# Four conditional parts instead of two arms for seven of the eight experts, and every block sends its own output

## The chip, the cores and the metric

One core of a Trainium2 chip runs the kernel. The time is what the device needs for one execution, in microseconds, as the median of several runs. Beside the timed runs there is one profiled execution, from which all rows below are taken. PE is the matrix engine (TensorE), PEld its weight loads, DVE is VectorE, ACT is ScalarE, POOL is GpSimd and SP is SyncE, which here only starts transfers.

## The reference

The work is a chunked attention, a dense two-layer network and a mixture of eight experts, one after the other. The change touches the mixture alone:

```python
    logits = x @ w_gate
    expert_idx = np.argmax(logits, axis=1)
    ...
    gate_w = probs[np.arange(N), expert_idx]
    ...
        if counts[e] < capacity:
            disp[e, counts[e]] = x[i]
            ...
    h = np.maximum(np.einsum('ecd,edf->ecf', disp, w1), 0.0)
    y = np.einsum('ecf,efd->ecd', h, w2)
    ...
            out[i] = gate_w[i] * y[expert_idx[i], pos[i]]
```

N is 1536 tokens, D 512, F 1024, and the capacity of an expert 384 tokens. So an expert has up to three blocks of 128 tokens. How many tokens it really gets is known only when the kernel runs.

## The kernel before, in words

Every f32 operand is held as a high and a low part, and a product is made of three matmuls (high by high, high by low, low by high). The experts run in the order of `EORDER`; the number e below counts in that order, from 0. The first expert (e = 0) has code of its own (`after_first`, L990), which the change does not restructure. For e = 1 to 7 the loop at L1245 writes two arms under `tc.If(cnt[EORDER[e]] > P)` (L1260):

- The arm `more` (L1006) is for over 128 tokens. `layer1` (L847) runs for eight pieces of F over both blocks together: 96 matmuls of 256 columns, each piece evacuated by ACT (L861, the high part of `hT`) and then by DVE (L862, the low part). `next_trans` (L974) then transposes both blocks of the next expert on PE (L825, 8 transposes), which ACT (L829) and DVE (L830) copy out as the high and low part of `xs`. `layer2(0)` follows: 24 matmuls of 512 columns (L925). Then comes `rest(2)` (L958) with a second `tc.If` (L963): over 256 tokens, the arm transposes block 2, runs `layer2(1)` and then the whole of block 2 (`block`, L866); else the arm runs `layer2(1)` alone.
- The arm `one` (L985) is for up to 128 tokens: `block(0)` with its 24 matmuls of 512 columns in layer 1 (L880), eight transposes of `hs` (L889), 24 matmuls of layer 2 (L925), and `next_trans` in its midst.

The last block of either arm does not send its result. It leaves it in one PSUM tile, copies its gate and its rows' numbers to two small tiles on POOL (L938, L939), and `after_arms` (L955) behind both arms sends it: ACT scales it (L945) and POOL starts an indirect transfer (L946). An earlier block of an arm sends its own.

In the same arms the weights of the coming steps are split into their high part (ACT, L289) and low part (DVE, L294), eight pieces for each expert: four of this expert's w2 and four of the next expert's w1. In `more` the eight stand in one stretch of code with layer 1, in `one` they stand between the steps of the block.

Which expert takes which arm can be read from the trace by the tiles: e = 1 takes `more` with block 2 (365.32 to 402.24 us), e = 2 takes `one` (405.14), e = 3 `more` (419.82), e = 4 `one` (444.63), and e = 5, 6 and 7 take `more` (461.56, 485.12, 508.75).

Order and waits: a planner (Tile) orders the instructions of one arm freely by their priorities, but moves nothing into or out of an arm. Each engine runs its own instruction stream, with its own branch at each condition, and counts its finished work in one counter of its own; who needs a result waits until the counter of its producer has reached a number. The numbers go on through the program as it is written. An arm that is not taken leaves a hole in them, and the engine itself fills it: where it passes such an arm without other work in it, it first waits until its own earlier work is done and then adds the missing count in one step. For the two arms of one If and Else the numbers run side by side, and the first instruction of the shorter arm adds the difference.

On PE a matmul is two instructions, a weight load and a multiplication. In the text of the program the arm `more` up to L963 has 256 such instructions, the arm of L963 168, its else 48, and `one` 128.

Of the kernel before, what the change touches and what calls it, by code (L numbers as in the profile page):

```python
# [9 lines left out]
F32 = mybir.dt.float32  # L10
# [3 lines left out]
I32 = mybir.dt.int32  # L14
# [7 lines left out]
P = 128  # L22
# [21 lines left out]
EORDER = (1, 2, 0, 3, 4, 5, 6, 7)  # L44
# [43 lines left out]
def kernel(  # L88
# [14 lines left out]
    nc = tc.nc  # L103
# [246 lines left out]
    def w_state():  # L350
        return w_at[0], list(flight), list(free_slots), list(free_raw), dict(where), set(ready)
# [46 lines left out]
    def psum(kind, name):  # L398
        pool, tag, shape = ps_pools[kind]
        return pool.tile(shape, F32, tag=tag, name=name)  # L400
# [399 lines left out]
    def expert_parts(e, ep, tp, cnt):  # L800
# [32 lines left out]
        def gate(b):  # L833
            sm = tp.tile([P, 1], F32, tag="gs", name="gs")
            nc.scalar.activation(out=tp.tile([P, E], F32, tag="ex", name="ex"), in_=xr[b][:, DM:DM + E], func=AF.Exp, accum_out=sm)  # L835
            g = tp.tile([P, 1], F32, tag="gt", name="gt", bufs=8)
            nc.vector.tensor_scalar(out=sm, in0=sm, scalar1=EPS, scalar2=None, op0=ALU.add)
            nc.vector.reciprocal(out=g, in_=sm)
            gt[b] = g

        def hT_of(b):
            key = 0 if b < 2 else b
# [23 lines left out]
        def block(b, last, pump=lambda i: None, between=None):  # L866

            with in_order():
# [42 lines left out]
                pump(5)  # L911
                layer2_part(b, p2, range(4, F2))
                pump(6)
            evacuate(b, p2, last)

        def y_of(last):
            return ylast[0] if last else psum("y", "psy")

        def layer2_part(b, ps, fcs):
            h = hT[0 if b < 2 else b]  # L920
# [7 lines left out]
        def layer2(b, last):  # L928
            ps = y_of(last)
            layer2_part(b, ps, range(F2))  # L930
            evacuate(b, ps, last)

        ylast = []

        def evacuate(b, ps, last):
            if last:

                nc.gpsimd.tensor_copy(ylast[1], gt[b])  # L938
                nc.gpsimd.tensor_copy(ylast[2], taker[:, b, ex:ex + 1])  # L939
            else:  # L940
                send(ps, gt[b], taker[:, b, ex:ex + 1])

        def send(ps, g, place):
            y = ep.tile([P, DM], F32, tag="y", name="y", bufs=2)
# [4 lines left out]

        def before_arms():  # L950
            hT_of(0)
            ylast.extend([psum("yl", "psy"), tp.tile([P, 1], F32, tag="gl", name="gl"),
                          tp.tile([P, 1], I32, tag="tl", name="tl")])

        def after_arms():  # L955
            send(*ylast)

        def rest(b):  # L958

            if b == NCB:  # L960
                layer2(b - 1, True)
                return
            with tc.If(cnt[ex] > b * P) as more:  # L963
                trans(b)
                layer2(b - 1, False)
                gate(b)
                later(b)
            with more.Else():
                layer2(b - 1, True)

        def later(b):
            block(b, True)

        def next_trans():  # L974
            if e + 1 < E:
                parts[e + 1].trans(0)
                parts[e + 1].trans(1)
# [28 lines left out]
        def more():  # L1006

            for b in range(2, NCB):
                load(b)
            for fc in range(F2):  # L1010
                mm, act = layer1(fc)
                if fc == GFC:
                    after_act = act
                if fc == TFC:
                    after_mm = mm
                if fc in PUMPS:
                    w_next(e)
            with tc.issue_after(after_act):
                for b in range(2):
                    gate(b)  # L1020
            with tc.issue_after(after_mm):
                next_trans()
            layer2(0, False)
            with tc.high_priority(offset=-LOWER2):
                while w_next(e):
                    pass
            rest(2)
        return SimpleNamespace(load=load, trans=trans, xs_of=xs_of, one=one, more=more, after_first=after_first,
                               before_arms=before_arms, after_arms=after_arms)


    with ExitStack() as st:
# [187 lines left out]
    with ExitStack() as st:  # L1220
# [24 lines left out]
        for e in range(E):  # L1245
            if e + 1 < E:
                for b in range(2):
                    parts[e + 1].load(b)
                parts[e + 1].xs_of(0)
            if e == 0:  # L1250
                with tc.high_priority(offset=LOADS):
                    w_loads(8 * (F // 512))
                first_block.send()
                parts[0].after_first()
            else:
                parts[e].before_arms()
                with tc.high_priority(offset=LOADS):
                    w_loads(8 * (F // 512))
                before = w_state()
                with tc.If(cnt[EORDER[e]] > P) as full:  # L1260
                    parts[e].more()
                after = w_state()
                w_back(before)
                with full.Else():
                    parts[e].one()
                assert w_state() == after
                parts[e].after_arms()
            for j in range(F // 512):
                w_free(("w1", e, j))
            for j in range(F // 512):  # L1270
                w_free(("w2", e, j))
# [70 lines left out]
```

## Time and profile before

| | |
|---|---|
| median of 3 runs | 540.67 us (539.94 to 542.19) |
| profiled execution, its own time | 540.01 us |
| its span, first to last instruction | 538.2 us |
| time around the span | 1.8 us |
| PE busy | 516.9 us (96%) |
| DVE, ACT, POOL busy | 311.0, 272.6, 85.1 us |
| mean granted clock of PE | 0.991 |

Of the profile, the busy shares and the forty slices say which engine sets the pace; the table of stretches says the same for each expert; the timeline of PE shows where it stands still (the idle time before a line, and who ended it, in square brackets); a line's own view shows the branch and counter instructions of each engine's sequencer (PEldq, ACTq and so on), with the shortest, median and longest duration in ns.

### The profile page before, as it was taken

How to read it: one execution, taken by the hardware profiler on the slowest of the kernel's cores; microseconds unless marked ns; L12 is line 12 of the kernel's file. 1: busy time of each engine (PE TensorE's matmuls, PEld its weight loads, DVE VectorE, ACT ScalarE, POOL GpSimd, SP SyncE). 2: the span in 40 equal slices, each digit the busy share in tenths (PEclk: the TensorE clock that was granted, in tenths of full speed). 3: DMA queues.
4: the chain of work that ended last, by engine and by line, in shares of the span. 5: the costliest groups of instructions: out<-in, count | busy, mean ns of one | idle time of the engine just before them, and what ended most of it. 6: DMA issues, size and time to landing. Idle time of an engine off the chain costs nothing. (4 is left out here: it accounts for less than half of the span.)

```text
span 538.2 us, 10665 instructions
## 1 busy us (share of the span) xinstructions
PE 516.9 (96%) x4211; PEld 445.0 (83%) x4211; DVE 311.0 (58%) x627; ACT 272.6 (51%) x551; POOL 85.1 (16%) x92
## 2 busy tenths in 40 slices
PE   8898999999999999999999999999988997999995
PEld 4686888899988999889988887779777976989893
DVE  4899799995229722228375446457314944947250
ACT  2786879773237422235254334457235925938231
POOL 3211012222001100004100000232022222201111
PEclk9999999999999999999999999999998998999999
DMA  8985654342003530000168213597524884885000
GB/s 287 328 315 193 238 174 141 120 158 79 1 0 119 184 130 1 1 0 2 37 210 264 80 41 98 161 319 260 181 62 160 269 324 146 279 328 196 23 26 31
DMA packets 38955, 80.29 MB, mean 149 GB/s; under 512 B 4009, under 2 KB 10153, under 8 KB 38890
## 3 DMA queue, kind: packets, MB, share of 16 engines
q1 hardware_dynamic: 36010, 70.66, 38.3%
q0 software_dynamic: 2880, 8.74, 5.1%
q8 instruction: 43, 0.70, 0.5%
q14 instruction: 22, 0.18, 0.1%
HBM read 69.90 MB, written 10.27 MB: 149 GB/s over the span
## 5 line engine op out<-in xcount | busy, mean ns | idle before, releaser
L584 PE MATMUL acc<-w,g 128*128 128x512 f32 x576 | 153.3, 400 | 1.1 <-DVE w L294 0.7
L541 PEld LDWEIGHTS psh<-xT,w 128*128 128x128 f32 x1152 | 146.7, 188 | 7.4
L541 PE MATMUL psh<-xT,w 128*128 128x256 f32 x1152 | 151.1, 280 | 0.0
L584 PEld LDWEIGHTS acc<-w,g 128*128 128x128 f32 x576 | 100.6, 188 | 21.5 <-issue 2.1
L556 ACT ACTIVATE sg<-psh 128x256 f32<-128x256 f32 x96 | 36.8, 384 | 128.2 <-PE psh L541 127.8
L294 DVE TENSOR_TENSOR w<-raw,w 128x1024 fp32r<-128x1024 f32 x64 | 77.2, 1220 | 41.5 <-ACT w L289 38.0
L564 DVE TENSOR_TENSOR g<-sg,g 128x256 fp32r<-128x256 f32 x87 | 40.3, 463 | 77.8 <-ACT g L560 74.7
L925 PE MATMUL psy<-w,hT 128*128 128x512 f32 x336 | 82.7, 400 | 0.3 <-ACT y L945 0.3
L925 PEld LDWEIGHTS psy<-w,hT 128*128 128x128 f32 x336 | 62.0, 188 | 15.3 <-ACT y L945 0.6
L289 ACT ACTIVATE w<-raw 128x1024 fp32r<-128x1024 f32 x64 | 66.3, 1060 | 2.8 <-PE acc L584 2.2
L858 PEld LDWEIGHTS psh<-xs,w 128*128 128x128 f32 x480 | 58.0, 188 | 1.1 <-issue 0.7
L858 PE MATMUL psh<-xs,w 128*128 128x256 f32 x480 | 58.3, 282 | 0.3 <-PEq L1000 0.3
L560 ACT ACTIVATE g<-psh 128x256 fp32r<-128x256 f32 x96 | 36.2, 380 | 0.0
L595 DVE SCALAR_TENSOR_TENSOR x<-acc,x 128x512 f32<-128x512 f32 x36 | 24.3, 687 | 18.2 <-PE acc L584 18.0
L880 PE MATMUL psh<-w,xs 128*128 128x512 f32 x96 | 27.4, 438 | 7.0 <-ACT w L289 2.9
L880 PEld LDWEIGHTS psh<-w,xs 128*128 128x128 f32 x96 | 19.6, 210 | 12.7 <-issue 7.2
L808 POOL DMA_INDIRECT xr<-rows,taker x20 | 24.2, 1211 | 23.6 <-DVE w L294 16.9
L294 DVE TENSOR_TENSOR w<-w,w 128x512 fp32r<-128x512 f32 x27 | 21.6, 802 | 9.5 <-ACT w L289 9.3
L270 DVE SCALAR_TENSOR_TENSOR w<-raw,w 128x512 int32<-128x512 int32 x32 | 23.4, 734 | 0.1
L259 ACT ACTIVATE w<-raw 128x512 f32<-128x512 f32 x32 | 21.1, 670 | 1.4 <-DMA raw<-in_w_out_dram 1.2
L289 ACT ACTIVATE w<-w 128x512 fp32r<-128x512 f32 x32 | 20.0, 628 | 3.5 <-POOL w L284 2.0
L284 POOL TENSOR_TENSOR w<-w,rest 128x512 int32<-128x512 int32 x8 | 12.1, 1507 | 60.8 <-DVE w L270 55.0
(134 smaller groups left out, 487.2 us busy)
## 6 DMA issues: line engine op xcount, KB each, us to landing
raw<-in_w_dram SPq DMA_DIRECT2D x64, 512.0 KB, 5.0
raw<-in_w_in_dram SPq DMA_DIRECT2D x16, 512.0 KB, 3.8
raw<-in_w_out_dram SPq DMA_DIRECT2D x16, 512.0 KB, 3.3
vt<-in_v_dram SPq DMA_DIRECT2D x12, 512.0 KB, 3.6
kt<-in_k_dram SPq DMA_DIRECT2D x12, 368.0 KB, 6.7
qt<-in_q_dram SPq DMA_DIRECT2D x12, 256.0 KB, 4.1
out_dram<-blank SPq DMA_DIRECT2D x12, 256.0 KB, 4.2
rows<-x SPq DMA_DIRECT2D x5, 520.0 KB, 4.1
```

Source lines behind the costliest of these rows:

```text
L289: nc.scalar.activation(out=w_dst(self.name, self.i, 0), in_=w, func=AF.Copy)
L294: eng.tensor_tensor(out=lo, in0=w, in1=hi.bitcast(F32), op=ALU.subtract)
L541: nc.tensor.matmul(ps, lhsT=w[:, wz, c, i * P:(i + 1) * P], rhs=xT[tb][:, xz, c, :], start=n == 0, stop=n == 3 * KC - 1)
L556: nc.scalar.activation(out=sg_t[u], in_=h_t[u], func=AF.Silu, scale=1.702)
L560: g_last[:1] = [nc.scalar.activation(out=g[:, 0], in_=h_t.pop(u), func=AF.Silu, scale=1.702).ins]
L564: lo = eng.tensor_tensor(out=g[:, 1], in0=sg_t.pop(u), in1=g[:, 0].bitcast(F32), op=ALU.subtract)
L584: nc.tensor.matmul(acc_t[tb][s], lhsT=g[:, gz, s * P:(s + 1) * P], rhs=w[:, wz, wi, :], start=i == 0 and n == 0, stop=u == last_of(k, tb) ...
L595: nc.vector.scalar_tensor_tensor(out=dst, in0=acc_t[tb][s], scalar=1 / 1.702, in1=dst, op0=ALU.mult, op1=ALU.add)
L808: return nc.gpsimd.indirect_dma_start(out=t, out_offset=None, in_=rows[:, :], in_offset=bass.IndirectOffsetOnAxis(ap=taker[:, b, ex:ex + 1 ...
L858: mm = nc.tensor.matmul(ps, lhsT=w[:, wz, c, f0:f0 + P], rhs=t[:, xz, c, :], start=m == 0, stop=m == 3 * KC - 1)
L880: nc.tensor.matmul(p1[j], lhsT=x[:, xz, c, o:o + P], rhs=w[:, wz, c, :], start=(xz, wz, c) == (0, 0, 0), stop=(xz, wz, c) == (1, 0, KC - 1))
L925: nc.tensor.matmul(ps, lhsT=h[:, hz, fc, o:o + P], rhs=w[:, wz, fc % 4, :], start=fc == 0 and n == 0, stop=fc == F2 - 1 and n == 2)
```

## The change

The two arms of e = 1 to 7 become four conditional parts in a row, none of them with an Else:

1. over 128 tokens: `more`, now only layer 1, the gates and `next_trans`;
2. up to 128 tokens: `one`, as it was;
3. over 128 tokens: `more2`, that is `layer2(0)`, the rest of the weights and `layer2(1)`;
4. over 256 tokens: `rest`, that is the transposes, the gate and the whole of block 2.

Each block sends its own output in its own part, so `ylast`, `after_arms` and the two copies on POOL go. The tiles for the gates are made ahead of the parts (`gt_of`). Six of the eight weight pieces of an expert with over 128 tokens now stand in `more2`, two in `more`.

```diff
-            g = tp.tile([P, 1], F32, tag="gt", name="gt", bufs=8)
+            if b not in gt:
+                gt_of(b)
...
         def y_of(last):
-            return ylast[0] if last else psum("y", "psy")
+            return psum("yl" if last else "y", "psy")
...
-        def evacuate(b, ps, last):
-            if last:
-
-                nc.gpsimd.tensor_copy(ylast[1], gt[b])
-                nc.gpsimd.tensor_copy(ylast[2], taker[:, b, ex:ex + 1])
-            else:
-                send(ps, gt[b], taker[:, b, ex:ex + 1])
+        def evacuate(b, ps):
+            send(ps, gt[b], taker[:, b, ex:ex + 1])
...
-        def after_arms():
-            send(*ylast)
-
-        def rest(b):
-
-            if b == NCB:
-                layer2(b - 1, True)
-                return
-            with tc.If(cnt[ex] > b * P) as more:
-                trans(b)
-                layer2(b - 1, False)
-                gate(b)
-                later(b)
-            with more.Else():
-                layer2(b - 1, True)
-
-        def later(b):
-            block(b, True)
+            for b in range(NCB):
+                gt_of(b)
...
+        def more2():
+
             layer2(0, False)
             with tc.high_priority(offset=-LOWER2):
                 while w_next(e):
                     pass
-            rest(2)
+            layer2(1, True)
+
+        def rest():
+
+            for b in range(2, NCB):
+                with tc.If(cnt[ex] > b * P):
+                    trans(b)
+                    gate(b)
+                    block(b, b % 2 == 1)
...
-                with tc.If(cnt[EORDER[e]] > P) as full:
+                with tc.If(cnt[EORDER[e]] > P):
                     parts[e].more()
+                middle = w_state()
+                w_back(before)
+                with tc.If(cnt[EORDER[e]] < P + 1):
+                    parts[e].one()
                 after = w_state()
-                w_back(before)
-                with full.Else():
-                    parts[e].one()
+                w_back(middle)
+                with tc.If(cnt[EORDER[e]] > P):
+                    parts[e].more2()
                 assert w_state() == after
-                parts[e].after_arms()
+                parts[e].rest()
```

`w_state` and `w_back` only keep the book of the weight tiles while the program is written: `one` and `more2` write and read the same tiles.

## Rows read from the trace of the kernel before

**Rows 1.** The page: busy time of the engines; PE's granted clock in 40 slices.

```profile
PE 516.9 (96%) x4211; PEld 445.0 (83%) x4211; DVE 311.0 (58%) x627; ACT 272.6 (51%) x551; POOL 85.1 (16%) x92
...
PEclk9999999999999999999999999999998998999999
```

**Rows 2.** Stretches, PE alone: length, busy (matmuls), granted clock, DMA share, GB/s.

```profile
405.14:409.40 4.26, 4.26 (x12) 0.60 0.60 189
...
419.82:443.62 23.80, 23.80 (x153) 1.00 0.90 307
443.62:447.38 3.76, 0.47 (x1) 0.95 0.38 109
447.38:450.40 3.02, 3.02 (x8) 0.50 0.78 227
...
485.12:508.75 23.63, 23.63 (x153) 1.00 0.37 124
```

**Rows 3.** Timeline of PE: start, length, instructions, idle time before and its releaser.

```profile
365.32 11.69 PE L858 MATMUL psh<-xs,w 128*128 128x256 f32 x96 [0.32 <-PEq L1000]
...
390.00 4.36 PE L880 MATMUL psh<-w,xs 128*128 128x512 f32 x18
...
405.14 5.99 PE L880 MATMUL psh<-w,xs 128*128 128x512 f32 x18 [2.91 <-ACT w L289]
...
444.63 0.47 PE L880 MATMUL psh<-w,xs 128*128 128x512 f32 x1 [1.01 <-ACT y L945]
447.38 5.47 PE L880 MATMUL psh<-w,xs 128*128 128x512 f32 x17 [2.28 <-issue]
```

**Rows 4.** Lines L1260 and L963: branches of PE's sequencer, ns min/median/max, first and last start.

```profile
L1260 PEldq COMPARE_BRANCH  x1: 5036/5036/5036, 399.9 to 399.9; - x1
...
L1260 PEldq COMPARE_BRANCH  x1: 2974/2974/2974, 441.5 to 441.5; - x1
...
L963 PEldq COMPARE_BRANCH  x10: 65/294/2167, 379.4 to 527.2; - x10
```

**Rows 5.** Waits of POOL: who waited for whom, total us, times, longest.

```profile
POOL out_dram L946 <- ACTq L963: 56.0, 4, 15.0
```

**Rows 6.** Timeline of all engines around the transposes for the next expert, e = 0.

```profile
361.15 1.03 PE L825 MATMUL pst<-ident,xr 128*128 128x128 f32 x8
361.79 1.09 ACT L829 ACTIVATE xs<-pst 128x512 fp32r<-128x512 f32 x2 [1.24 <-PE pst L825]
...
361.94 3.06 PE L925 MATMUL psy<-w,hT 128*128 128x512 f32 x12
362.42 1.29 DVE L830 TENSOR_TENSOR xs<-pst,xs 128x512 fp32r<-128x512 f32 x2 [0.95 <-ACT xs L829]
```

**Rows 7.** Timeline where layer 1 of the last expert (e = 7) ends.

```profile
520.18 11.40 PE L925 MATMUL psy<-w,hT 128*128 128x512 f32 x48
520.38 0.39 ACT L861 ACTIVATE hT<-psh 128x256 fp32r<-128x256 f32 x1 [1.03 <-PE psh L858]
520.80 0.42 DVE L862 SCALAR_TENSOR_TENSOR hT<-psh,hT 128x256 fp32r<-128x256 f32 x1 [0.99 <-ACT hT L861]
```

**Rows 8.** Timeline where the two `one` experts end (e = 2, then e = 4).

```profile
418.88 5.76 DVE L294 TENSOR_TENSOR w<-raw,w 128x1024 fp32r<-128x1024 f32 x5
...
420.61 0.69 ACT L945 ACTIVATE y<-psy,gl 128x512 f32<-128x512 f32 x1
...
460.60 5.77 DVE L294 TENSOR_TENSOR w<-raw,w 128x1024 fp32r<-128x1024 f32 x5
461.56 8.67 PE L858 MATMUL psh<-xs,w 128*128 128x256 f32 x71
```

**Rows 9.** Timeline at the start of block 2 of e = 1.

```profile
383.34 0.60 PE L825 MATMUL pst<-ident,xr 128*128 128x128 f32 x4
383.54 0.69 ACT L945 ACTIVATE y<-psy,gt 128x512 f32<-128x512 f32 x1 [4.97 <-PE psy L925]
...
384.31 0.59 ACT L829 ACTIVATE xs<-pst 128x512 fp32r<-128x512 f32 x1
```

More of the change, by code (lines that the diff above doesn't have):

```diff
@@ L835, in gate, with gt_of @@
             nc.scalar.activation(out=tp.tile([P, E], F32, tag="ex", name="ex"), in_=xr[b][:, DM:DM + E], func=AF.Exp, accum_out=sm)
-            g = tp.tile([P, 1], F32, tag="gt", name="gt", bufs=8)
+            if b not in gt:
+                gt_of(b)
             nc.vector.tensor_scalar(out=sm, in0=sm, scalar1=EPS, scalar2=None, op0=ALU.add)
-            nc.vector.reciprocal(out=g, in_=sm)
-            gt[b] = g
+            nc.vector.reciprocal(out=gt[b], in_=sm)
+        def gt_of(b):
+            gt[b] = tp.tile([P, 1], F32, tag="gt", name="gt", bufs=9)
         def hT_of(b):
@@ L913, in block @@
                 pump(6)
-            evacuate(b, p2, last)
+            evacuate(b, p2)
         def y_of(last):
-            return ylast[0] if last else psum("y", "psy")
+            return psum("yl" if last else "y", "psy")
         def layer2_part(b, ps, fcs):
@@ L930, in layer2 @@
             layer2_part(b, ps, range(F2))
-            evacuate(b, ps, last)
-        ylast = []
-        def evacuate(b, ps, last):
-            if last:
-                nc.gpsimd.tensor_copy(ylast[1], gt[b])
-                nc.gpsimd.tensor_copy(ylast[2], taker[:, b, ex:ex + 1])
-            else:
-                send(ps, gt[b], taker[:, b, ex:ex + 1])
+            evacuate(b, ps)
+        def evacuate(b, ps):
+            send(ps, gt[b], taker[:, b, ex:ex + 1])
         def send(ps, g, place):
@@ L951, in before_arms @@
             hT_of(0)
-            ylast.extend([psum("yl", "psy"), tp.tile([P, 1], F32, tag="gl", name="gl"),
-                          tp.tile([P, 1], I32, tag="tl", name="tl")])
-        def after_arms():
-            send(*ylast)
-        def rest(b):
-            if b == NCB:
-                layer2(b - 1, True)
-                return
-            with tc.If(cnt[ex] > b * P) as more:
-                trans(b)
-                layer2(b - 1, False)
-                gate(b)
-                later(b)
-            with more.Else():
-                layer2(b - 1, True)
-        def later(b):
-            block(b, True)
+            for b in range(NCB):
+                gt_of(b)
         def next_trans():
@@ L1026, in more @@
                     pass
-            rest(2)
-        return SimpleNamespace(load=load, trans=trans, xs_of=xs_of, one=one, more=more, after_first=after_first,
-                               before_arms=before_arms, after_arms=after_arms)
+            layer2(1, True)
[5 more added lines that the diff above has]
+                    block(b, b % 2 == 1)
+        return SimpleNamespace(load=load, trans=trans, xs_of=xs_of, one=one, more=more, more2=more2, rest=rest,
+                               after_first=after_first, before_arms=before_arms)
     with ExitStack() as st:
```

## The prediction

> **What bounds the kernel now.** I read the page first, then the stretches, the timeline of PE, the branches, and last who waits for whom. The page says that PE is busy for 96% of the span, the next engine for 58%, and that the granted clock is full but for two dips [rows 1]. So only what stops or slows PE counts. The stretches show where the experts lose: one with over 128 tokens loses nothing (23.80 us busy of 23.80, 23.63 of 23.63), while the entry into the second `one` expert is 3.76 us with a single matmul in it, followed by 3.02 us at half clock; after the entry into the first `one`, 4.26 us have a mean clock of 0.60 [rows 2]. The timeline gives the idle times: 2.91 us ahead of the first `one` (e = 2); 1.01 and 2.28 us around the one matmul ahead of the second (e = 4) [rows 3]. The clock costs more on top: 18 of these matmuls take 4.36 us at full clock (0.242 each) and 5.99 us after the first stop, so 1.6 us; 17 take 5.47 us after the second, where 4.1 would do, so 1.4 us [rows 3]. The two entries together: 6.2 us idle and 3.0 us of slow clock, 9.2 us.
>
> What stops PE there is no missing result, though the profile names ACT: the weights and `xs` of these experts were made during the expert before. PE's own branch at L1260 took 5.04 us at e = 2 and 2.97 us at e = 4, while its ten branches at L963 take 0.07 to 2.17 us, half of them under 0.3 [rows 4]. Both long ones jump over the whole arm `more`, 472 PE instructions as counted in the program; the ordinary ones jump over 130 to 170. [...]
>
> **The change part by part.** I add to the profiled execution, 540.0 us; the median of the runs shown is 0.7 us higher.
>
> *Shorter jumps.* The way into `one` now leads over `more` without its second half, 208 instructions, and then past empty parts. That is nearer to the ordinary jumps than to the 472, so I take their cost (a median of 0.29 us [rows 4], spent while earlier matmuls still run) and remove all 9.2 us. Bounds: nothing removed, and all of it. What is late next is a wait: `one` is preceded by `more` passed over, and PE's first matmul takes a PSUM tile last read in `more`, so it needs ACT's count for that part. ACT passes it only after it has scaled the last output, about 0.15 + 0.69 us after PE's end (the wait of 1.01 us that is there already [rows 3] has this length). I put 1.0 us at each of the two entries, 2.0.
>
> *The wait between the two halves.* This is the main term. `layer2(0)` reads `hT`. Before, only `more` wrote it ahead of `layer2(0)`. Now `one` is written between them in the program and writes the same `hT` and the same weight tiles, so the wait of `layer2(0)` is for numbers of ACT and DVE that belong to `one`. Where `one` isn't taken, ACT and DVE add these numbers when they have passed it, after all of their work in `more`. That such a count is waited for shows before: POOL waited 56.0 us in four waits for ACT's sequencer at L963, a condition and no work [rows 5]. The last work in `more` is copying the transposes of `next_trans`. Before, 24 matmuls of layer 2 ran on while this was done; behind the matmuls that now wait stand all of layer 2 and the next expert. Counted from the first transpose at 361.15, ACT is done at 362.88 (+1.73) and DVE at 363.71 (+2.56), while PE went on with other matmuls at 361.94 (+0.79) [rows 6]. With 0.1 us for the signal PE can run one matmul (0.24) at +1.83, as it needs only high parts, and the rest from +2.66: 2.66 - 0.79 - 0.24 = 1.6, which I round up to 1.7 for the branch. Four experts (e = 1, 3, 5, 6): 6.8. The last has no next expert: ACT's L861 ends at 520.77, DVE's L862 at 521.22, PE went on at 520.18 [rows 7]: 1.04 + 0.1 - 0.24 = 0.9. Sum 7.7. Bounds: 0.3 each (only the empty part, next term), 1.5 in all; and 3.0 each, 15, if one of DVE's 1.1 us weight pieces [rows 8] is still queued ahead of the copies.
>
> *The way out of `one`.* The next expert's layer 1 reads w1, which `more2` writes as well, later in the program than `one`. So PE now waits until ACT and DVE have passed `more2`, after their whole work in `one`. At PE's end, 419.82 (the start of layer 1 of e = 3 [rows 2]), ACT still has its output to scale, to 421.30. DVE has five pieces queued from 418.88 in 5.76 us, of which three are of `one`: done at 422.3, 2.5 us after PE's end; at e = 4 three of five from 460.60 are done at 464.1, against a start of layer 1 at 461.56 [rows 8]: 2.5 us again. Before, PE didn't wait for them, because the first matmuls need only the first piece. Twice 2.5: 5.0. Bounds: 0.3 each and, if ACT scales the output ahead of the last pieces, 4.0 each. A stop of 2.5 us is near the two that were followed by a slow clock, which cost 1.4 to 1.6 us each: I add one, 1.5, with bounds of none and two.
>
> *Block 2 of e = 1.* Its transposes took 0.60 us from 383.34, and layer 2 of block 1 then covered ACT's scaling (383.54, 0.69 us) and its copy of `xs` (384.31 to 384.90) [rows 9]. Now layer 2 of block 1 is over, so block 2 stands for about 1 us between its transposes and the end of the copy, less the 0.3 us that PE stood there anyway: 0.7.
>
> *Empty parts.* From e = 5 to 6 and from 6 to 7 PE now passes the fourth part with nothing in it: it lets its own matmuls end, adds the count and branches. The one such place before cost 0.32 us [rows 3]; with the restart of the weight loads I take 0.4, twice 0.8. At the other passages this lies inside the waits above. [...]
>
> *Costed at nothing.* The two POOL copies go, off PE's path. The sends stand in the parts: POOL's transfers for a later expert's tokens lie behind them now, but tokens are fetched more than one expert ahead, and one expert lasts 23.6 us [rows 2]; if that cover were gone, `next_trans` would stop PE by the missing time. SP's weight loads for six of eight pieces start some 10 us later, since DVE frees the buffers later; they have the length of the next expert's layer 1 as cover, and a miss would show as ACT waiting for `raw`. The end of the kernel (last matmul, scaling, transfer) keeps its order.
>
> Sum: 540.0 - 9.2 + 2.0 + 7.7 + 5.0 + 1.5 + 0.7 + 0.8 = 548.5; with the 0.7 us up to the median, 549.2. I predict 549.
>
> **The rivals.**
> *Faster: the halves aren't held.* If the waits of `more2` and of the layer 1 after `one` were settled by the real producers, only the empty parts remain (5 × 0.4 and 2 × 0.4, and 0.4 twice at the way out): 540.0 - 9.2 + 2.0 + 2.0 + 0.8 + 0.8 + 0.7 + 0.7 = 537.8. For it: each single matmul before waits for the piece of `hT` that it reads. Against it: the count on which POOL waits [rows 5], and PE's own wait for its sequencer at an empty part (0.32 us, PEq L1000). Chance 0.13.
> *The same: ACT's count alone decides.* If DVE passed early, each wait is that for ACT: 1.73 + 0.1 - 0.79 = 1.0 five times, and 1.5 twice: 540.0 - 9.2 + 2.0 + 5.0 + 3.0 + 0.7 + 0.8 + 0.7 = 543.0. Against it: DVE's copies are the low parts that the third matmul needs. Chance 0.10.
> *Much slower: each passed part is a late jump.* An empty part lets PE run dry before it branches, so a jump that was hidden behind running matmuls stands open. At 2.17 us, the longest of L963 [rows 4], five jumps over `one` would add 2.2 - 0.3 each (part of it beside the wait: 5 us in all) and the seven ends of experts 1.9 each, 13 us, with some slow clock: some 567 us. It decides if the code behind a part of 100 to 130 instructions is not there yet. Against it: half of the ten branches of L963, of the same reach, took under 0.3 us. [...] Chance 0.12.
> *The change doesn't do what it says:* the way into `one` stays as slow as it was, the rest comes as forecast: 549.2 + 7.2 = 556. Within the range; it shares the forecast's sign.
>
> **How the numbers follow.** The forecast with its bounds has 0.65, of which 0.10 is the slow entry: slower in all, with the much slower case, 0.77. What can be told from no change here is about 0.5%, 2.7 us: 538.0 to 543.4. Faster 0.13, same 0.10. The range leaves out the faster rival and the late jumps' far end: from 542, the lower bounds of the waits (1.5 for 7.7 would be 543.0), to 558, the slow entry and a second slow clock.
>
> **What would show it right or wrong.** Right: in the timeline PE stands 1.5 to 2 us between layer 1 (L858, L825) and layer 2 (L925) of e = 1, 3, 5 and 6, released by ACT or DVE at the new conditions; about 2.5 us ahead of layer 1 of e = 3 and 5; about 1 us ahead of L880 of e = 2 and 4, without the 2.28 us of "issue"; PE's branches all under 0.4 us. Wrong: no idle time ahead of `layer2(0)` (the faster rival); branches of over 2 us at the new conditions (late jumps); ACT waiting for `raw` or PE for `xr` (the covers that I counted on).

## The result and the profile after

| | before | after |
|---|---|---|
| median, same chip | 540.31 us (4 runs, 538.75 to 542.19) | 547.73 us (4 runs, 547.01 to 548.93) |
| ratio | | 1.0138 (95%: 1.0099 to 1.0177) |
| profiled execution, its own time | 540.01 us | 548.29 us |
| its span | 538.2 us | 546.5 us |

The change costs 7.4 us; 549.0 was forecast. The page of the changed kernel (busy time of the engines, PE's granted clock in 40 slices):

```profile
PE 518.2 (95%) x4207; PEld 443.5 (81%) x4211; DVE 316.5 (58%) x627; ACT 277.0 (51%) x551; POOL 80.7 (15%) x78
...
PEclk9899999999999999999999999999999999999999
```

The clock's dips of before, in the second half [rows 1], are gone; the time went elsewhere. The new lines: L1249, L1253, L1257 and L1012 are the conditions of the four parts, L861 is layer 1 of `more` (L858 before), L883 layer 1 of a block (L880), L928 layer 2 (L925).

The longest item of what made PE wait, from 345 us to the end (total us, times, longest). `ACTq L1253` is ACT's sequencer at the condition of `one`: a condition, not a result:

```profile
PE psy L928 <- ACTq L1253: 3.6, 5, 0.8
```

And the timeline of PE where its stops stand (start, length, instructions, idle time before and its releaser); e = 1 from 367.29, e = 2 from 407.01, e = 3 from 421.73, e = 4 from 449.09, e = 6 from 490.61, e = 7 from 516.55:

```profile
367.29 11.69 PE L861 MATMUL psh<-xs,w 128*128 128x256 f32 x96 [0.32 <-PEq L977]
378.81 1.04 PE L825 MATMUL pst<-ident,xr 128*128 128x128 f32 x8
380.63 0.50 PE L928 MATMUL psy<-w,hT 128*128 128x512 f32 x1 [0.78 <-ACTq L1253]
381.48 11.28 PE L928 MATMUL psy<-w,hT 128*128 128x512 f32 x47 [0.35 <-DVEq L1253]
392.60 0.60 PE L825 MATMUL pst<-ident,xr 128*128 128x128 f32 x4
394.26 4.47 PE L883 MATMUL psh<-w,xs 128*128 128x512 f32 x18 [1.06 <-ACT xs L829]
...
402.15 4.44 PE L928 MATMUL psy<-w,hT 128*128 128x512 f32 x18
407.01 4.44 PE L883 MATMUL psh<-w,xs 128*128 128x512 f32 x18 [0.42 <-PEq L1249]
...
417.28 3.04 PE L928 MATMUL psy<-w,hT 128*128 128x512 f32 x12
421.73 0.50 PE L861 MATMUL psh<-xs,w 128*128 128x256 f32 x2 [1.40 <-ACTq L1257]
422.80 11.54 PE L861 MATMUL psh<-xs,w 128*128 128x256 f32 x94 [0.57 <-DVEq L1257]
...
436.85 11.27 PE L928 MATMUL psy<-w,hT 128*128 128x512 f32 x47 [0.35 <-DVEq L1253]
449.09 4.45 PE L883 MATMUL psh<-w,xs 128*128 128x512 f32 x18 [0.97 <-ACTq L1012]
...
478.93 11.25 PE L928 MATMUL psy<-w,hT 128*128 128x512 f32 x47 [0.35 <-DVEq L1253]
490.61 11.75 PE L861 MATMUL psh<-xs,w 128*128 128x256 f32 x96 [0.43 <-PEq L1012]
...
516.55 11.67 PE L861 MATMUL psh<-xs,w 128*128 128x256 f32 x96 [0.43 <-PEq L1012]
528.74 11.75 PE L928 MATMUL psy<-w,hT 128*128 128x512 f32 x48 [0.52 <-ACTq L1253]
```

Three things are to be seen. The entries into `one` (407.01 and 449.09) have lost their long stops and their slow clock: 18 matmuls take 4.44 and 4.45 us at a granted clock of 1.00, where the first entry took 5.99 [rows 3]. In each `more` that has a next expert PE stops after the transposes, lets one matmul of layer 2 run, stops again and goes on. And behind each `one` layer 1 of the next expert stops in the same two steps.

The difference of the profiled executions, 8.3 us, is made up so: e = 1 starts 1.97 us later (367.29 against 365.32 [rows 3]); that arises in the first 20 us, in the attention, in code that the change doesn't touch. PE's granted clock was 0.81 in a part of it in this execution (the stretch below: length, PE busy, granted clock, DMA share, GB/s) and 1.00 in the execution before; how much of the 1.97 us is the clock's isn't shown:

```profile
15.00:24.00 9.00, 6.17 (x110) 0.81 1.00 373
```

From there to PE's end it is 173.20 us (540.49) against 166.26 (531.58), +6.94. Behind it the end is 0.6 us shorter. So +6.94 is what the change did in this execution.

What PE waits for in the middle shows in the timeline of ACT and DVE at e = 1:

```profile
379.45 1.09 ACT L829 ACTIVATE xs<-pst 128x512 fp32r<-128x512 f32 x2
380.08 1.29 DVE L830 TENSOR_TENSOR xs<-pst,xs 128x512 fp32r<-128x512 f32 x2 [0.22 <-ACT xs L829]
```

ACT ends its copies at 380.54 and PE's one matmul starts at 380.63; DVE ends at 381.37 and the other 47 start at 381.48. But those copies are the `xs` of the *next* expert. Layer 2 doesn't read them; it waits until the two engines have got past `one`, which each does only when its own work is over: their counter instructions at L1253 stand at 380.6 (ACT) and 381.4 us (DVE).

### The profile page after: what moved, and what is told of

It reads as the page before. It is cut to its first block, busy times and chain, and to the rows that moved or that the text cites. A ratio compares the mean times of both kernels' runs of the same rounds, so it can differ in the third digit from the quotient of the medians.

```text
span 546.5 us, 11048 instructions
## 1 busy us (share of the span) xinstructions
PE 518.2 (95%) x4207; PEld 443.5 (81%) x4211; DVE 316.5 (58%) x627; ACT 277.0 (51%) x551; POOL 80.7 (15%) x78
## 5 line engine op out<-in xcount | busy, mean ns | idle before, releaser
L294 DVE TENSOR_TENSOR w<-raw,w 128x1024 fp32r<-128x1024 f32 x64 | 75.7, 1222 | 33.0 <-ACT w L289 28.7
L928 PE MATMUL psy<-w,hT 128*128 128x512 f32 x336 | 83.8, 401 | 5.1 <-ACTq L1253 3.6
L928 PEld LDWEIGHTS psy<-w,hT 128*128 128x128 f32 x336 | 62.1, 188 | 22.2 <-ACTq L1253 4.8
L289 ACT ACTIVATE w<-raw 128x1024 fp32r<-128x1024 f32 x64 | 64.4, 1051 | 10.4 <-DVEq L1253 3.8
L861 PE MATMUL psh<-xs,w 128*128 128x256 f32 x480 | 59.2, 283 | 5.1 <-ACTq L1257 2.8
L861 PEld LDWEIGHTS psh<-xs,w 128*128 128x128 f32 x480 | 57.8, 188 | 7.6 <-ACTq L1257 3.7
L942 POOL DMA_INDIRECT out_dram<-y,taker x14 | 16.3, 1164 | 141.3 <-ACT y L941 71.7
L865 DVE SCALAR_TENSOR_TENSOR hT<-psh,hT 128x256 fp32r<-128x256 f32 x40 | 16.5, 423 | 25.6 <-ACT hT L864 21.3
L864 ACT ACTIVATE hT<-psh 128x256 fp32r<-128x256 f32 x40 | 15.2, 383 | 31.6 <-PE psh L861 30.5
L883 PE MATMUL psh<-w,xs 128*128 128x512 f32 x96 | 24.4, 403 | 3.3 <-ACT xs L829 1.9
L808 POOL DMA_INDIRECT xr<-rows,taker x20 | 22.6, 1130 | 28.5 <-DVE w L294 16.9
L941 ACT ACTIVATE y<-psy,gt 128x512 f32<-128x512 f32 x14 | 9.5, 681 | 33.7 <-issue 14.5
L883 PEld LDWEIGHTS psh<-w,xs 128*128 128x128 f32 x96 | 17.5, 188 | 8.2 <-ACT xs L829 2.4
```

The source lines that it names most:

```text
L289: nc.scalar.activation(out=w_dst(self.name, self.i, 0), in_=w, func=AF.Copy)
L294: eng.tensor_tensor(out=lo, in0=w, in1=hi.bitcast(F32), op=ALU.subtract)
L808: return nc.gpsimd.indirect_dma_start(out=t, out_offset=None, in_=rows[:, :], in_offset=bass.IndirectOffsetOnAxis(ap=taker[:, b, ex:ex + 1 ...
L861: mm = nc.tensor.matmul(ps, lhsT=w[:, wz, c, f0:f0 + P], rhs=t[:, xz, c, :], start=m == 0, stop=m == 3 * KC - 1)
L883: nc.tensor.matmul(p1[j], lhsT=x[:, xz, c, o:o + P], rhs=w[:, wz, c, :], start=(xz, wz, c) == (0, 0, 0), stop=(xz, wz, c) == (1, 0, KC - 1))
L928: nc.tensor.matmul(ps, lhsT=h[:, hz, fc, o:o + P], rhs=w[:, wz, fc % 4, :], start=fc == 0 and n == 0, stop=fc == F2 - 1 and n == 2)
```

## The experiments

Theory: PE waits for *numbers*. A tile that a passed part writes too is waited for by the number of its last writer in the program, and a passed part's number is added only when the engine's earlier work is done. Rival: it is the splitting itself, with more conditions, branches and drains, that costs. For the time that came back, the theory was shorter jumps; the rival, that the stop belongs to `one`. The kernels fall into four groups by what they ask: the halves, the way out, the empty part, the jumps. Each ratio is to the kernel before, run beside it, whose medians were 541.79 to 542.12 us.

### The halves: the second one beside nothing that `one` writes

```diff
-                with tc.If(cnt[EORDER[e]] > P):
+                with tc.If(cnt[EORDER[e]] > P) as full:
                     parts[e].more()        # now with all eight weight pieces
...
-                with tc.If(cnt[EORDER[e]] < P + 1):
+                with full.Else():
                     parts[e].one()
...
                 with tc.If(cnt[EORDER[e]] > P):
                     parts[e].more2()       # layer 2 alone
```

> `more` (layer 1, transposes, all eight weight pieces) and `one` as If and Else, then the second half (layer 2 only) under a condition of its own, then `rest`. The second half is still a separate part with a condition, but it writes nothing that another arm writes out of step, and its weight pieces are made before it. Theory: the stop in the middle goes (only the short drain, 0.3 to 0.5 us each), the one behind `one` too, the jump into `one` stays as short as in the changed kernel: 540.0 - 9.2 + 1.4 (entries) + 5 x 0.4 (middle) + 0.9 (empty ends) + 0.7 (block 2 of e=1) = 535.8 on the scale of the profiled runs, about 536.5 median, 0.992 of the kernel before and 0.979 of the changed one. Rival (splitting `more` in two costs the 7.7 us whoever writes what): 543 or more.

Measured: 540.02 us, 0.9971 of the kernel before (0.9947 to 0.9996). Timeline of PE of this kernel: the middle of e = 1, the entry to e = 2, the way out of it:

```profile
378.37 1.04 PE L825 MATMUL pst<-ident,xr 128*128 128x128 f32 x8
379.16 11.48 PE L928 MATMUL psy<-w,hT 128*128 128x512 f32 x48
...
400.03 4.44 PE L928 MATMUL psy<-w,hT 128*128 128x512 f32 x18
404.31 4.38 PE L883 MATMUL psh<-w,xs 128*128 128x512 f32 x18
...
418.91 0.38 PE L861 MATMUL psh<-xs,w 128*128 128x256 f32 x1 [1.35 <-ACTq L1256]
```

The second half is still a part of its own with its own condition, and there is no stop ahead of it: 0.79 us from the transposes to layer 2, as before the change [rows 6]. So the split is free, and the rival falls for the halves. The stop behind `one` did not go, though the theory said it would. It costs 2.5 us at each of its two places, 5.0 us in all, while the middle, put at 2.0, cost nothing; so the total missed 536.5 by 3.5 us. Why the stop is there is the question of the group on the way out.

### The halves: `one` written last

```diff
                 with tc.If(cnt[EORDER[e]] > P):
                     parts[e].more()
...
+                with tc.If(cnt[EORDER[e]] > P):
+                    parts[e].more2()
...
                 with tc.If(cnt[EORDER[e]] < P + 1):
                     parts[e].one()
...
-                with tc.If(cnt[EORDER[e]] > P):
-                    parts[e].more2()
```

> Four parts as in the changed kernel, in another order: both halves of `more` one behind the other, then `one`, then `rest`. Theory (a consumer waits for the number of the LAST writer in the program, also of a part that is passed over; the changed kernel loses 7.7 us so between the halves and 4.5 us behind `one`): no stop of PE between layer 1 and layer 2 of e = 1, 3, 5, 6 and 7 (-7.7), and none of 1.4 + 0.6 us behind `one` (-4.5). In exchange `one` is the last writer of weights and hT for every expert with over 128 tokens: at e=5 to 6 and 6 to 7 PE waits for ACT and DVE to end their part, 1 to 2.5 us instead of 0.43, so +1 to +4. The way into `one` leads over some 305 PE instructions, between 208 (which was short) and 472 (which was long): 0 if it is near, up to +9 with slow clock if it is far. So against the 548 of the changed kernel 538 to 541 if the jump is near, 541 to 548 if it is far. Rival (any split into more parts with own conditions costs PE its drain and branch, whoever writes what): the stop between layer 1 and layer 2 stays at 1.6 us five times, about 548.

Measured: 543.36 us, 1.0026 (1.0004 to 1.0047). Timeline of PE: e = 1, e = 4, e = 6; and the two branches of PE's sequencer ahead of e = 4 (ns, shortest, median and longest; first and last start):

```profile
379.90 1.04 PE L825 MATMUL pst<-ident,xr 128*128 128x128 f32 x8
380.69 11.66 PE L928 MATMUL psy<-w,hT 128*128 128x512 f32 x48
...
448.79 5.99 PE L883 MATMUL psh<-w,xs 128*128 128x512 f32 x18 [3.59 <-PEq L1251]
...
489.13 11.75 PE L861 MATMUL psh<-xs,w 128*128 128x256 f32 x96 [1.06 <-ACTq L1255]
```

```profile
L1012 PEldq COMPARE_BRANCH  x1: 220/220/220, 445.4 to 445.4; - x1
...
L1249 PEldq COMPARE_BRANCH  x1: 2027/2027/2027, 445.9 to 445.9; - x1
```

With the same four parts and no other writer between the halves the stop is gone too (0.79 us again). As forecast, another took its place where `one` is now passed last: 1.06 us ahead of e = 6. A passed part alone doesn't make such a stop: ahead of e = 6 of the changed kernel the part for block 2 is passed too, which writes no weights, and there PE only drains (0.43 us, `PEq`). One of the two entries became a late jump, 2.03 us, with a stop of 3.59 us and 5.99 us for the 18 matmuls behind it: near at one entry, far at the other, and the total lies in the range given for a far jump.

### The halves: less work to wait for

```diff
-            with tc.issue_after(after_mm):
-                next_trans()               # in more()
...
             layer2(0, False)
+            next_trans()                   # in more2()
```

> The changed kernel with one step moved: the transposes of the next expert's tokens stand no longer at the end of `more`, but in `more2` behind layer2(0). Theory (PE waits in the middle until ACT and DVE have ended ALL their work of the first half, whatever it is): at e = 1, 3, 5 and 6 the last work of that half is now the copy-out of hT, as it already is at e = 7, so the stop shrinks from 1.64 us of lost PE time to the 1.1 of e = 7: 4 x 0.5 = 2 us faster than the changed kernel, 545.7. Rival (the stop is the price of the branch and the drain): stays at 1.6 us each, 547.7.

Measured: 547.84 us, 1.0105 (1.0064 to 1.0146). Timeline of PE at e = 3 and at e = 6:

```profile
436.50 0.50 PE L928 MATMUL psy<-w,hT 128*128 128x512 f32 x1 [0.30 <-ACT w L289]
437.76 2.83 PE L928 MATMUL psy<-w,hT 128*128 128x512 f32 x11 [0.76 <-DVE w L294]
...
490.74 11.75 PE L861 MATMUL psh<-xs,w 128*128 128x256 f32 x96 [0.43 <-PEq L1011]
503.01 6.13 PE L928 MATMUL psy<-w,hT 128*128 128x512 f32 x24 [0.52 <-ACTq L1252]
```

The stop itself shrank, as expected: at e = 6 it is 12.27 us from layer 1 to layer 2, where 96 matmuls without a stop take 11.52 (367.29 to 378.81 in the changed kernel), and the first 24 matmuls of layer 2 take 6.13 us, where the second 24 take 5.86: 1.0 us lost instead of 1.64, with 1.1 expected. That supports the theory; a price of branch and drain would not have moved. In the profiled execution two other things took the gain back: layer 2 of e = 3 now came too early for its weights (0.30 and 0.76 us), with ACT waiting 2.58 us for SP, whose loads stand behind the condition, and layer 1 of e = 5 took 13.04 us for 95 matmuls, where that of e = 3 took 11.66. For the total this run is inconclusive: 1.0105 against the 1.0138 of the changed kernel, with intervals that overlap.

### The way out of `one`: the two arms again, block 2 behind them

```diff
-                with tc.If(cnt[EORDER[e]] > P):
+                with tc.If(cnt[EORDER[e]] > P) as full:
                     parts[e].more()
+                    parts[e].more2()
...
-                with tc.If(cnt[EORDER[e]] < P + 1):
+                with full.Else():
                     parts[e].one()
...
-                with tc.If(cnt[EORDER[e]] > P):
-                    parts[e].more2()
...
                 parts[e].rest()
```

> The two arms If and Else of the kernel before, but block 2 taken out of `more` into a part of its own behind both arms, and each block sends its own output (so the halves of `more` are one arm again). Theory: no wait in the middle and none behind `one`, because the numbers of the two arms run side by side: -7.7 and -4.5 against the changed kernel's 548, +0.5 at most at each of the seven empty or taken `rest` parts. The way into `one` leads over some 305 PE instructions: 535 to 537 if that is near (no stop of 2 us, no slow clock), 541 to 545 if it is far as in the kernel before. Rival (the split of the third block and the separate sends cost as much as the halves): no better than 545.

Measured: 540.71 us, 0.9974 (0.9957 to 0.9991). Timeline of PE at the first entry and behind that `one`:

```profile
403.42 4.38 PE L883 MATMUL psh<-w,xs 128*128 128x512 f32 x18
...
417.09 0.36 PE L861 MATMUL psh<-xs,w 128*128 128x256 f32 x1 [0.43 <-PEq L1012]
419.08 13.15 PE L861 MATMUL psh<-xs,w 128*128 128x256 f32 x95 [1.64 <-DVEq L1012]
```

The entries are free of late jumps, with 308 instead of 472 PE instructions in the arm that is jumped over: no idle time at e = 2, 0.78 us at e = 4. But behind `one` PE stands 1.64 us more, for DVE. No part that writes weights is passed there, so the theory as I had put it (last writer in a *passed* part) didn't cover this. The text of the program gave the refinement: the numbers of If and Else run side by side and end alike, and a reader behind both waits for the larger of a tile's two numbers. In `more` the copy of `xs` is now DVE's *last* work; in `one` three weight pieces follow it. So layer 1 would wait for a number that in `one` belongs to the third of these pieces. The profile names DVE's sequencer at the condition of block 2 instead (`DVEq L1012`), which DVE passes right behind that piece; the kernels with the copies, below, tell the two apart. In the kernel before, the arm ended with block 2, more DVE work stood behind `xs`, and nothing was waited for. The next two kernels are this one with three tiny DVE copies added to `more`, of which nothing is read, behind `xs` or ahead of it.

```diff
...
+            pad = tp.tile([P, 1], F32, tag="pad", name="pad")
+            for _ in range(3):
+                nc.vector.tensor_copy(pad, ps[:, :1])   # behind layer2(1)
```

> The two-arm kernel with block 2 in a part of its own, plus three tiny DVE copies (128x1) at the very end of `more`, which nothing reads. In the version without them the first matmuls of layer 1 behind `one` wait for the DVE number that the copy of `xs` has in `more`, which there is DVE's last work; side by side it is also the last number of `one`, where three weight pieces follow `xs`, so PE stands 1.64 us twice (and got a slow clock of 1.5 us once). Theory (only the numbers count): with three operations behind `xs` in `more` as well, the number of `xs` is the same in both arms, and the 1.64 us stops vanish: 2 x (1.64 + 0.2) + 1.5 = 5.2 us less than the 540.7 of that version, 535.5; 3.7 less, 537, if its slow clock was chance. Rival (PE really needs what DVE does last in `one`, or DVE is simply late): no change, 540 to 541.

Measured: 535.5 us, 0.9897 (0.9862 to 0.9931). Ahead of `xs` (the copies read `gt[0]` and stand before the transposes):

> Control for the three tiny DVE copies: the same two-arm kernel with block 2 in a part of its own, and the same three copies in `more`, but ahead of the copies of `xs`, so that these are again DVE's last work in `more`. Theory (only the numbers count): the stops of 1.64 us behind `one` are there again, 540 to 541 as without the copies (0.997 of the kernel before). Rival (three more DVE operations in `more` help in another way, say by DVE's pace): 535.5 to 537, as with the copies at the end.

Measured: 540.95 us, 0.9992 (0.9964 to 1.002). Timeline of PE behind the first `one`, with the copies behind `xs`:

```profile
417.64 11.77 PE L861 MATMUL psh<-xs,w 128*128 128x256 f32 x96 [0.32 <-PEq L1017]
```

and with the copies ahead of it:

```profile
418.83 11.66 PE L861 MATMUL psh<-xs,w 128*128 128x256 f32 x95 [1.64 <-DVEq L1015]
```

The same three operations, and 5 us between the two places. More work in an arm that isn't even taken here took the stop away, because it moved a number. Nor did layer 1 need the third piece itself: with the copies behind `xs` DVE ended the third piece at 419.70 us, 2.06 us after layer 1 had begun. And DVE passes the part for block 2 in all three kernels, so that isn't what PE waits for. That is the theory in its narrowest form.

### What an empty part costs

The kernel with the copies behind `xs`, and an Else for the third block:

```diff
-                with tc.If(cnt[ex] > b * P):
+                with tc.If(cnt[ex] > b * P) as third:
...
+                with third.Else():
+                    nc.tensor.transpose(psum("t", "pst")[:, :P], ident, ident)
```

> As the kernel with the three tiny DVE copies, and the third block's condition gets an Else arm with one transposition of the identity on PE, which nothing reads. Theory (a part without an Else makes PE drain its own matmuls before it passes, 0.43 us idle and 0.2 of refilling at each of five passages, e = 2 to 6; with an Else the first instruction there adds the count and nothing is drained): the idle time `<- PEq` of the new condition vanishes or falls under 0.1 us, 5 x 0.5 = 2.5 us less than the version without the Else: about 533 to 534.5. Rival (the 0.43 us is the price of the jump itself): no change against the version without the Else.

Measured: 532.53 us, 0.9834 (0.9798 to 0.9869): the fastest of all, 1.7% under the kernel before. Timeline of PE between e = 5 and e = 6, and the branches at the first condition and at that of block 2 (ns, shortest, median, longest):

```profile
467.95 11.46 PE L928 MATMUL psy<-w,hT 128*128 128x512 f32 x48
479.25 0.27 PE L1022 MATMUL pst<-ident 128*128 128x128 f32 x1
479.28 11.98 PE L861 MATMUL psh<-xs,w 128*128 128x256 f32 x96
```

```profile
L1256 PEldq COMPARE_BRANCH  x12: 70/172/3461, 367.7 to 522.0; - x12
...
L1017 PEldq COMPARE_BRANCH  x8: 73/276/3554, 387.5 to 522.3; - x8
```

No idle time is left at any of the passages of block 2, where 0.32 to 0.78 us stood. Two branches took 3.46 us (at the entry to e = 4) and 3.55 us (from e = 5 to e = 6) here, the length of those that cost so much before. Without a drain PE still had matmuls queued: the first made it 0.23 us late, the second not at all.

### The jumps: the arms swapped in the kernel before

```diff
-                with tc.If(cnt[EORDER[e]] > P) as full:
-                    parts[e].more()
+                with tc.If(cnt[EORDER[e]] < P + 1) as small:
+                    parts[e].one()
...
-                with full.Else():
-                    parts[e].one()
+                with small.Else():
+                    parts[e].more()
```

> The kernel before, with its two arms swapped: `one` is the If arm and stands first, `more` the Else arm behind it. Theory (the stops ahead of `one` are late jumps: PE's code behind a jump over 472 instructions, right behind another jump, isn't there yet): the way into `one` no longer leads over `more`, so no branch of over 2 us and no stop of 2 to 3 us ahead of L880 of e = 2 and 4; instead the way OUT of `one` leads over all of `more`: a branch of 2 to 5 us and a stop of 2 to 4 us, followed by a slow clock, ahead of layer 1 of e = 3 and 5. In all about the time of the kernel before, 0.99 to 1.01 of it. Rival (the stop belongs to `one` itself, its first weights or its code, not to what is jumped over): the stops stay ahead of L880 of e = 2 and 4.

Measured: 552.73 us, 1.0241 (1.0168 to 1.0314). Timeline of PE: the entry to e = 2, its way out, the way out of e = 4; and the branches (shortest, median, longest):

```profile
403.42 4.38 PE L880 MATMUL psh<-w,xs 128*128 128x512 f32 x18
...
425.06 13.05 PE L858 MATMUL psh<-xs,w 128*128 128x256 f32 x96 [8.39 <-issue]
...
470.28 14.17 PE L858 MATMUL psh<-xs,w 128*128 128x256 f32 x96 [6.96 <-issue]
```

```profile
L1260 PEldq COMPARE_BRANCH  x9: 73/334/6394, 366.3 to 515.8; - x9
```

The stop moved from the entry to the exit, and with it the slow layer 1 (96 matmuls in 13.05 and 14.17 us, where e = 1 takes 11.70), so it belongs to the jump over `more` and not to `one`. Its size was underrated: 8.4 and 7.0 us, not 2 to 4, and the total is 2.4% up instead of level.

### The jumps: a part that is never taken

The changed kernel with one part more ahead of `one` of e = 4, holding 60 transpositions (120 PE instructions) or 160 (320):

```diff
+                if e == 4:
+                    with tc.If(cnt[EORDER[e]] > NT - 1):
+                        dead = psum("t", "dead")
+                        for _ in range(60):
+                            nc.tensor.transpose(dead[:, :P], ident, ident)
```

> The changed kernel with a part that is never taken put ahead of `one` of e = 4; it holds 60 transpositions, 120 PE instructions. So PE passes 208 (`more`) and 120 instructions right behind each other. Theory (what counts is how much code is passed in a row without a stop in which the next could be fetched): 328 in a row is about the 330 (122 + 208) that took one branch of 2.0 us in the kernel with `one` last, and the 308 of the two-arm kernel took 0.43: at the border, +0.3 us at the entry if near, +2 if not. Rival (each jump counts alone, by its own length): 208 and 120 are both under every short jump so far, so +0.3 us and no branch over 0.5 us.

> The same with 160 transpositions, 320 PE instructions, in the part that is never taken: 528 in a row. Theory (code passed in a row): at least one branch of over 2 us in PE's sequencer, the idle time ahead of L883 of e = 4 grows from 0.97 to 3 to 6 us, and layer 1 of the block may run at half clock, 6.0 instead of 4.4 us for 18 matmuls. Rival (the stops before the change had another reason than the code passed): +0.3 us at most.

Measured (one run each): 559.93 and 555.2 us. Timeline of PE at the entry to e = 4 with 60, the branch at the new condition; then the same entry with 160:

```profile
456.71 6.95 PE L883 MATMUL psh<-w,xs 128*128 128x512 f32 x18 [6.15 <-PEq L1254]
```

```profile
L1254 PEldq COMPARE_BRANCH  x1: 4976/4976/4976, 451.3 to 451.3; - x1
```

```profile
451.93 6.95 PE L883 MATMUL psh<-w,xs 128*128 128x512 f32 x18 [5.83 <-PEq L1254]
```

Both are late, and alike. A jump over 120 instructions, shorter than any late one so far, took 4.98 us: it came right behind the jump over 208 (330 ns from 450.7 us on). So the length of a single jump doesn't decide; a short one can be late right behind another. The two-arm kernel's 308, 4 us behind the jump before, were near (0.43 us, the first row below, at its entry to e = 4); 120 + 208 and 208 + 120 in a row were late, and so were the 308 in the kernel with the Else (3.46 us), which there come 0.5 us behind the jump before.

```profile
L1249 PEldq COMPARE_BRANCH  x1: 425/425/425, 444.5 to 444.5; - x1
...
L1015 PEldq COMPARE_BRANCH  x8: 73/276/2991, 385.4 to 527.8; - x8
```

But the amount that is passed in a row is not the whole rule. From e = 5 to e = 6 PE jumps past `one` and then past block 2, and from e = 6 to e = 7 the same two jumps follow each other. With the Else the second of them took 3.55 us at the first place and 0.35 at the other. With the three copies ahead of `xs` it took 2.99 us at the first place (the second row, its longest), with the copies behind `xs` 0.23. Every edit here also shifts where the code lies, which no run separates from how much is passed.

The DMA queues for instructions carry something at such branches: within the 4.98 us of the late branch above one packet of 0.02 MB came. In the kernel before, three packets (0.04 MB) came in the first 1.0 us of its branch of 5.04 us [rows 4], from 399.9 us on, and none in the 4.0 us after; in the 33 us from 366 us on there were three. What a late branch waits for, no run shows. In these kernels it took 1.5 to 6.4 us.

## Why the prediction was right, point by point

From start to start in the timelines of before and after (the idle time alone leaves out the refilling of the weight loads):

| step of the prediction | forecast | measured |
|---|---|---|
| shorter jumps | -9.2 | -9.8 |
| count of ACT at the entries | 2.0 | 0.6 + 1.2 |
| wait between the halves | 7.7 | 4 x 1.64 + 1.1 = 7.7 |
| way out of `one` | 5.0 | 2 x 2.4 = 4.8 |
| slow clock after it | 1.5 | 0 |
| block 2 of e = 1 | 0.7 | 0.72 |
| empty parts | 0.8 | 1.2 |
| rest, by difference (small restarts, rounding) | | 0.5 |
| sum on the profiled execution | +8.5 | +6.9 |

**Shorter jumps.** All of it came, and the swapped arms show that it belongs to the jump. Two rows of before, not shown yet, give the starts:

```profile
397.79 4.45 PE L925 MATMUL psy<-w,hT 128*128 128x512 f32 x18
...
432.13 11.49 PE L925 MATMUL psy<-w,hT 128*128 128x512 f32 x48
```

To e = 2 (405.14 [rows 3]) it is 7.35 us, where the side-by-side kernel needs 4.28 (400.03 to 404.31): 3.1. At e = 4 it is 15.25 us to the second matmul (447.38 [rows 3]), where 48 matmuls take 11.30 (467.95 to 479.25 in the kernel with the Else) and one 0.24: 3.7. With 3.0 of slow clock, 9.8. The reason given, that 208 is "nearer to the ordinary jumps", was incomplete. At e = 4 the jump over 208 comes behind the one past block 2, with a drain of 4 us between them; in the kernel with the Else, which has no drain there, the jump behind block 2 was late (3.46 us). So that this entry became near was in part luck. One more small part in a row, and the much slower rival ("each passed part is a late jump") came true at that place, with 6.15 us of idle time. That code was "not there yet", as the rival has it, no run shows. Its chance of 0.12 was not too high.

**Between the halves.** From 378.81 the second matmul should come at +0.79 + 0.24 without a stop and came at 381.48, +2.67: 1.64 lost; 1.7 was forecast. The 0.1 us that I put for the signal was my estimate; it was 0.09 (380.54 to 380.63) and 0.11 (381.37 to 381.48). At e = 7 it is 12.19 us from layer 1 to layer 2 against 11.43, and 11.75 for the 48 matmuls against 11.40 [rows 7]: 1.1, forecast 0.9. The order (ACT first, one matmul, then DVE) is the one forecast from [rows 6].

**Way out.** From the last 12 matmuls to layer 1 it took 4.45 us instead of 2.87 (416.95 to 419.82 before), then 1.07 for two matmuls of 0.12: 1.58 + 0.83 = 2.4. DVE's three pieces ended at 422.68 (the row below), and the 94 matmuls began at 422.80: the term was right in size and cause.

```profile
419.19 3.49 DVE L294 TENSOR_TENSOR w<-raw,w 128x1024 fp32r<-128x1024 f32 x3
```

The slow clock that I added to it is the term that failed in this execution: 94 matmuls took 11.54 us, at a granted clock of 1.00. It was not a wrong idea. In seven of the profiles here (the changed kernel, the three others with its way out, block 2 behind two arms with and without copies ahead of `xs`, and the halves side by side) a stop of this kind stands 14 times, and 6 times layer 1 ran some 1.5 us longer after it. "One of two, none to two" was the right sort of term.

**Entries, empty parts.** The second entry waits for ACT as forecast: from 436.85 to 449.09 it is 12.24 us, where 47 matmuls take 11.06, so 1.2. At the first only PE's own drain is left (4.86 us from 402.15 instead of 4.28: 0.6). The number that PE waits for is that of the part for block 2 (`ACTq L1012`), not, as the prediction had it, that of `more`; at the first entry block 2 had really run. The empty parts cost 0.6 each by the starts (478.93 to 490.61 is 11.68 us, less 11.06), not the 0.43 of idle time: the weight loads start anew behind the drain, too. PEld stood 0.84 us there, and its first load starts at 490.58, 0.03 us ahead of the first matmul.

**Costed at nothing.** Rightly in the changed kernel: no wait for `raw` or `xr` shows ahead of PE. With the transposes moved, the cover of the weight loads ran out at e = 3, as the prediction had named it, for 1.1 us. The sign that it named, ACT waiting, shows in the changed kernel too, but off PE's path: 1.0 us for `raw` and 1.2 us for SP's sequencer, where the kernel before has 0.4 us for `raw`.

**The other rivals.** "The halves aren't held" and "ACT's count alone" are out by the timeline: DVE's step of 0.35 or 0.57 us stands in every one of these stops but the last, at e = 7. "The change doesn't do what it says" is out by the entries.

What stays open: whether `hT` or the weight tiles hold the halves (both are written by `one`, and the experiments took both away together), and what makes a jump late (the code passed right before it isn't the whole rule), and what sets its 1.5 to 6.4 us.

## What to carry to other kernels

Count what is behind a condition by the *numbers* that a reader waits for: a passed part that writes what comes next costs what its engines still had to do (1.64 us a time between the halves here), and in an If with Else the last work of one arm lines up with the last work of the other, so let the results that the next stage needs first be followed by other work in both arms (535.5 us here, and 540.95 with the same work ahead of them). A passed part without an Else drains the engine, 0.6 us each here; with one useless instruction in an Else it doesn't. Keep parts that may be passed few in a row, and let queued matmuls cover the jump: branches of 3.5 us cost 0.2 us or nothing with matmuls still queued, and one of 5.0 us behind a drain made PE stand for 6.2.

## What the runs showed of the hardware that was not expected

- A jump can be late right behind another one: 0.43 us for 308 PE instructions after a 4 us pause and 3.46 without one, 2.03 for 208 behind 120, 4.98 for 120 behind 208, and up to 6.39 right behind a late jump over the 472 of `more`. It isn't the whole rule: the same two jumps in a row ended with 0.23 us in one kernel and 2.99 in another. Most of PE's branches here take 70 to 430 ns.
- After 6 of 14 stops of the same kind (about 2 us in two steps) layer 1 lost some 1.5 us. With block 2 behind two arms its 95 matmuls took 13.15 us after the first stop and 11.65 after the second; the granted clock was 0.50 in the 3 us from 419.08 us on.
- All twelve kernels run the same attention and dense network, and still e = 1 started between 365.24 and 368.38 us in the profiled executions. The 1.97 us of the profiled difference that lie ahead of e = 1 are within this scatter of 3 us; a change in the experts is better read from the start of e = 1 on.
